# Attention and a two-layer feed-forward on one core: heads of a pair split to float16 together, and a fourth batch moved from float32 to float16 products

## The chip, the cores and the metric

The kernel runs on one core of a Trainium2 chip. A core has a matrix engine (TensorE, PE in the profile, with its weight loads as PEld), a vector engine (VectorE, DVE), a scalar engine (ScalarE, ACT), a general engine (GpSimd, POOL) and SyncE (SP), which here issues every DMA. On-chip memory is SBUF with 128 rows (partitions); TensorE writes its sums to PSUM. The metric is the device time of one execution in microseconds. The kernel before takes 1048.26 us, the median of three runs (1047.59 to 1049.46).

## The reference

Attention over 8 batches, 8 heads, 576 positions and 64 dimensions, with a decay that grows with the positive part of `s`; its result, laid out as 4608 tokens of 512 values, goes through two matrix products with an ELU between them.

```python
scores = scale * np.matmul(q, k.transpose(0, 1, 3, 2))          # scale = 1/8
causal = np.triu(np.ones((S, S), dtype=bool), k=1)
cum = np.cumsum(np.maximum(s, 0.0), axis=-1)
bias = -(cum[:, :, :, None] - cum[:, :, None, :])
scores = np.where(causal, -1000000000.0, scores + np.minimum(bias, 0.0))
scores = scores - np.max(scores, axis=-1, keepdims=True)
attn = np.exp(scores)
attn = attn / (np.sum(attn, axis=-1, keepdims=True) + 1e-09)
x = np.matmul(attn, v)           # then transposed to [4608, 512]
h = x @ w_in                                                     # [512, 2048]
g = np.where(h > 0.0, h, np.exp(np.minimum(h, 0.0)) - 1.0)
out = g @ w_out                                                  # [2048, 512]
```

## The kernel before, in words

**Order of work.** The program records every operation with a priority, the engines that could do it (with a cost in ns for each), what it reads and what it writes. `Plan.issue` then lists the operations greedily: what can start earliest by its own costs goes first, ties go to the priority. So the order on each engine is fixed when the program is built, and each engine waits for semaphores in that order. While TensorE would have nothing to do in the first 60 us of its planned time, the list puts fillers in: transposes into an unused PSUM tile (L1501, `scratch`).

**Two ways through the attention.** Two heads make a pair, so each batch has four pairs. The 576 queries are a first block of 64 and four of 128. `pieces` (L1512) sets the order: the first 320 queries (the first block and blocks 0 and 1) of batches 0 to 3, then batches 4 to 7 whole, then blocks 2 and 3 of batches 0 to 3.

- *The float32 way* (`Low`: `prepare_low` L743, `scoring_low` L770, `weighing_low` L809) serves the first 320 queries of batches 0 to 3, 16 pairs. It loads q, k and v of a pair, multiplies q and k in float32 (L1050), turns the weights of the softmax with TensorE transposes (L818, L834), copies them out of PSUM (L423, L424) and multiplies them with v in float32 (L820, L849).
- *The float16 way* (`Unit`: `prepare` L927, `scoring` L1126, `weighing` L1163) serves the rest. A value is split into a float16 high part and a float16 remainder. A pair is three units here: the first 64 queries of both heads together, then head 0, then head 1. Each unit loads its k and q twice over on 128 rows (tiles `stk`, `stq`), splits them (L408 to L410 for the high part, `remainder` L1008 for the rest), has one DMA to put a copy of q's high part in the tile `q2` (L997) and one to put three rows for the decay under k's remainder (`k2`). The scales come from `group_values` (L867): it loads all of a batch's q and k once more in four pieces of 128x1152 (`sx`, L883 to L889), takes the peaks of them and of the values, and `scales_of` (L620) makes scales of them: DVE maxima, a product with the identity (`flat`, L640), a DVE maximum over it (L632), a product with ones (`every`, L643), and a copy (L645). The scores are two float16 products (`kh` with `qs`, `k2` with `q2`); the weights are turned by DMA transposes (L389, tile `T`) and multiplied with v (`av`, L1212).

In both ways DVE and ACT share the softmax (L1053, L1058), and the result goes by DMA to `x_dram`.

**The feed-forward.** The 4608 tokens go through it in 18 chunks of 256 (`moe_chunk`). A chunk loads its x from `x_dram` (`xc`) and splits it into `xh` (ACT, POOL or DVE, L408 to L410) and `xl` (L1357). Chunk 0 uses float32 products (L1377, L1431); the others take three float16 products in the place of one float32 product: L1381 for the first layer (`h`), 24 matmuls for two of the 16 column blocks, and L1438 for the second (`o`), 12 for two. Chunk 1 holds the end of batch 0's first 320 queries and part of batch 1's, chunk 4 ends those of batch 3, chunk 5 starts with batch 4, and chunks 7, 9 and 11 are the first to need batches 5, 6 and 7.

**Weights.** `load_unit` (L658) brings a 128x512 block as raw words and decodes it with ACT and DVE (L675 to L684), with a peak for each. `weight_scales` (L648) makes one scale for each of the two matrices; its spans in `peaks` are those of the first matrix, those of the second and, as the third, the values' peaks of all 16 float32 pairs (`A_LOW`, `N_CUT * NP + 1`), which the first chunks' x is scaled by. Only then can `split_unit` (L693) make the float16 parts `wp` of the weights, and only with those can chunk 1 start.

**Memory.** The float32 weights' places are used again: the values `va` of the float16 batches stand in the last part of the first group, then in `w_all[0]` and `w_all[1]` by turns; the tiles `T` have `w_all[2]` and `w_all[3]`.

The constants: `P` = 128, `HB` = 64, `CUT` = 2, `NP` = 4 pairs, `N_CUT` = 4, `TMAX` = 256.

## Time and profile before

| | before |
|---|---|
| median of three runs | 1048.26 us |
| profiled execution, its own time | 1049.36 us |
| its span in the trace | 1047.6 us |
| mean granted TensorE clock | 0.996 |
| TensorE busy | 1014.1 us, 97% |
| VectorE busy | 854.6 us, 82% |
| ScalarE busy | 696.6 us, 66% |
| GpSimd busy | 309.2 us, 30% |
| moved by DMA | 169.26 MB |

The profile comes from one execution. A row of the timeline has the start in us, the duration in us, the engine, the line of the program, the operation, the tiles (output, arrow, inputs), the shapes, and in square brackets the engine's idle time before it with the instruction that ended it. Matmul ends are modelled, so a row's duration can reach a little into the next row. A float32 product has two records and a transpose one.

### The profile page before, as it was taken

The numbers are of one execution on the slowest core, as the hardware profiler recorded it, in microseconds if no ns is written. First come the engines' busy times: TensorE is split into PE (matmuls) and PEld (weight loads), VectorE is DVE, ScalarE is ACT, GpSimd is POOL, SyncE is SP. The second block draws the span as 40 slices with busy tenths as digits, with TensorE's granted clock in tenths as the row PEclk, the third lists the DMA queues.
The fourth block names the chain that finished last, engine by engine and source line by source line (L and its number), as shares of the span: only waits on it lengthen the run. The fifth ranks groups of instructions, "written<-read, shape, count | busy, mean of one in ns | idle before, by whom it ended". The sixth has DMA issues, their size and how long they took to land.

```text
span 1047.6 us, 22165 instructions
## 1 busy us (share of the span) xinstructions
PE 1014.1 (97%) x7354; PEld 696.8 (67%) x7354; DVE 854.6 (82%) x2222; ACT 696.6 (66%) x1568; POOL 309.2 (30%) x545
## 2 busy tenths in 40 slices
PE   8879998999999999999999999999999999999998
PEld 7656764666666666666666766666666676767665
DVE  7898656988888988989998999889888888876232
ACT  4788677766776765667777766676666666765343
POOL 6343114123353332335354434123421122210000
PEclk9999999999999999999999999999999999999999
DMA  8999856458889886688758866876785856664000
GB/s 250 251 263 277 250 150 180 129 127 180 188 205 189 171 205 135 147 142 209 158 141 168 215 150 145 175 180 161 156 180 140 154 140 137 145 121 102 6 21 21
DMA packets 289843, 169.26 MB, mean 162 GB/s; under 512 B 205856, under 2 KB 263424, under 8 KB 289728
## 3 DMA queue, kind: packets, MB, share of 16 engines
q1 hardware_dynamic: 289728, 167.84, 68.6%
q8 instruction: 58, 0.95, 0.4%
q14 instruction: 57, 0.47, 0.2%
HBM read 98.99 MB, written 19.24 MB: 113 GB/s over the span
## 4 chain that ended last, share of the span: by engine, by line
PE 50%; DVE 3%; DMA 2%; issue 1%; SPq 1%; POOL 0%; ACT 0%; DVEq 0%; POOLq 0%
PE o L1438 21%; PE h L1381 20%; PE sc L1050 4%; PE av L1212 4%; DVE p L1111 1%; DMA stk<-in_kT_dram 0%; DMA T<-p 0%; DVE h L1413 0%; DVE p L1053 0%; DMA stq_None<-in_qT_dram 0%; SPq L389 0%; DMA stq<-in_qT_dram 0%; DMA q<-qs 0%; DVE qs L1008 0%; DMA xc<-x_dram 0%
## 5 line engine op out<-in xcount | busy, mean ns | idle before, releaser
L1381 PE MATMUL h<-xh,wp 128*128 128x256 f16 x2176 | 397.6, 274 | 6.0 <-DVE wp L699 3.4
L1438 PE MATMUL o<-wp,gg 128*128 128x512 f16 x1632 | 393.8, 379 | 0.0
L1381 PEld LDWEIGHTS <-wp 128*128 128x128 f16 x3264 | 318.7, 98 | 74.5 <-DVE wp L699 5.3
L1381 PE MATMUL h<-xl,wp 128*128 128x256 f16 x1088 | 297.7, 274 | 0.9 <-DVE xl L1357 0.9
L1438 PEld LDWEIGHTS <-gg 128*128 128x128 f16 x1632 | 158.3, 98 | 143.4
L1058 ACT ACTIVATE p<-p,mn 128x192 f32<-128x192 f32 (+1 forms) x224 | 139.7, 624 | 43.7 <-DVE mn L1053 40.8
L1111 DVE SCALAR_TENSOR_TENSOR p<-p,sm,p 128x512 f16<-128x512 f32 (+3 forms) x233 | 149.0, 666 | 5.5 <-ACT p L1107 4.2
L1393 ACT ACTIVATE g<-h,cs 128x512 f32<-128x512 f32 x136 | 93.1, 684 | 90.5 <-PE h L1381 89.8
L1413 DVE SCALAR_TENSOR_TENSOR h<-g,cs,h 128x512 f32<-128x512 f32 x136 | 102.0, 750 | 52.7 <-ACT g L1400 51.4
L1417 ACT ACTIVATE gg<-h 128x512 f16<-128x512 f32 x133 | 78.8, 592 | 60.9 <-DVE h L1413 57.8
L1053 DVE CUSTOM_DVE_ANT_0 p<-sc,maskw 128x192 f32<-128x192 f32 (+1 forms) x224 | 106.0, 484 | 15.4 <-PE sc L1050 10.2
L1420 DVE SCALAR_TENSOR_TENSOR gg<-h,gg 128x512 f16<-128x512 f32 x136 | 93.2, 685 | 18.2 <-ACT gg L1417 17.2
L1103 POOL TENSOR_SCALAR p<-p,sm 128x64 f16<-128x64 f32 (+3 forms) x80 | 52.3, 659 | 144.5 <-DVE sm L1064 68.5
L1107 ACT ACTIVATE p<-p,sm 128x512 f16<-128x512 f32 (+3 forms) x128 | 72.4, 588 | 18.0 <-issue 6.9
L1050 PE MATMUL sc<-kh,qs 128*128 128x192 f16 (+2 forms) x256 | 75.8, 300 | 1.3 <-DVE mn L1053 0.7
L1050 PE MATMUL sc<-k,q 128*128 128x192 f16 (+2 forms) x256 | 75.5, 299 | 0.8 <-DMA q<-qs 0.7
L1212 PEld LDWEIGHTS <-v 128*64 128x64 f16 x896 | 45.4, 110 | 20.2 <-issue 9.8
L1212 PE MATMUL av<-T,v 128*64 128x256 f16 (+5 forms) x896 | 58.6, 280 | 0.2 <-DMA T<-p 0.2
L408 POOL TENSOR_SCALAR v<-va,scales 128x320 f16<-128x320 f32 x37 | 22.4, 611 | 109.4 <-PE av L1212 91.3
L408 POOL TENSOR_SCALAR qs<-stq,scales 128x256 f16<-128x256 f32 (+1 forms) x36 | 25.2, 701 | 91.3 <-PE sc L1050 80.9
L1008 DVE SCALAR_TENSOR_TENSOR k<-stk,scales,kh 64x576 f16<-64x576 f32 x61 | 49.9, 819 | 0.5
L1400 ACT ACTIVATE g<-g 128x512 f32<-128x512 f32 x77 | 48.4, 628 | 2.0
(189 smaller groups left out, 1441.8 us busy)
## 6 DMA issues: line engine op xcount, KB each, us to landing
stk<-in_kT_dram SPq DMA_DIRECT2D x64, 288.0 KB
va<-in_vb_dram SPq DMA_DIRECT2D x32, 320.0 KB
sx<-in_qT_dram SPq DMA_DIRECT2D x32, 288.0 KB
sx<-in_kT_dram SPq DMA_DIRECT2D x32, 288.0 KB
raws<-in_w_in_dram SPq DMA_DIRECT2D x16, 512.0 KB
raws<-in_w_out_dram SPq DMA_DIRECT2D x16, 512.0 KB
out_dram<-ost SPq DMA_DIRECT2D x32, 256.0 KB
stq<-in_qT_dram SPq DMA_DIRECT2D x32, 256.0 KB
```

What stands on the lines that cost most here:

```text
L1050: pe_.matmul(view(sc.v[:, :cw]), l, r, start=n == 0, stop=n == len(pairs) - 1)
L1053: op(prio, [("DVE", 84 + dve_p(cw), lambda i=i, sc=sc: dve.tensor_tensor_reduce(pt.v[:, i * cw : (i + 1) * cw], sc.v[:, :cw], mv(i * cw, c ...
L1058: op(prio, [("ACT", 480 + w / 1.2, lambda: act.activation(pt.v[:, :w], pt.v[:, :w], AF.Exp, bias=mn.v[:, n - 1 : n], scale=-1.0, accum_out ...
L1107: ("ACT", 295 + n / 1.2, lambda part=part: act.activation(part(t16, 0), own(part), AF.Copy, scale=sm.v[:, r])),
L1111: ("DVE-SB", dve_2(n), lambda part=part: dve.scalar_tensor_tensor(part(t16, 1), own(part), sm.v[:, r], part(t16, 0), ALU.mult, ALU.subtract)),
L1212: pe_.matmul(av.v[w.h * HB : (w.h + 1) * HB, dst], w.values.v[:, w.h, kb, v], part(w, kb, m), start=kb == 0 and m == 0 and v == 0, stop=kb ...
L1381: pe_.matmul(columns(k), weight_part(f, 0, part)[1]()[:, c * P : (c + 1) * P], xx.v[:, c], start=(c == 0 and m == 0), stop=(c == NCB - 1 a ...
L1393: op(side, [("ACT", act_c(W) + (0 if native else 90), lambda: act.activation(g.v, hp.v, AF.Exp, scale=1.0 if native else by(3)))], [hp] + ...
L1413: op(side, [("DVE", dve_p(W), lambda: dve.scalar_tensor_tensor(hp.v, g.v, by(2 if sign[0] else 1), hp.v, ALU.mult, ALU.max))], [g, cs], [hp])
L1417: ("ACT", act_c(W), lambda: act.activation(gg.v[:, 0], hp.v, AF.Copy, scale=2.0**-DOWN)),
L1420: op(side, [("DVE", dve_p(W), lambda: dve.scalar_tensor_tensor(gg.v[:, 1], hp.v, 2.0**-DOWN, gg.v[:, 0], ALU.mult, ALU.subtract))], [hp, ( ...
L1438: pe_.matmul(acc[i].v, gg.v[:, g, at], weight_part(f, 1, part)[1](), start=(f == 0 and m == 0), stop=(f == NF - 1 and m == 2),)
```

## The change

1. **`N_LOW = 3`.** Only batches 0, 1 and 2 go the float32 way for their first 320 queries. Batch 3's go the float16 way, as a group of their own, with two query blocks in place of four.
2. **Scales.** Each batch of the float32 way gets a scale for its values by a `scales_of` of its own, and `weight_scales` no longer has the third span. A float16 group needs only its values' scale: the second loads of q and k (`sx`) and their peaks are gone.
3. **Heads of a pair split together.** `prepare_pair` loads a pair's k and q once, head 0 on rows 0 to 63 and head 1 on rows 64 to 127, takes a peak for each row (`pk`), makes a power of two for each row of q and its inverse for k, and splits all with one operation for each part of k and of q. `spread` then puts the parts with twelve DMAs from SBUF to SBUF, and the decay rows with a thirteenth, into a tile `set` with the four operands of the two score products for both heads. There are two such sets in turns; the second has the place of `w_all[1]`, so `va` has `w_all[0]` alone after the first group. `scoring` waits for all parts of the set.

The core of the diff:

```diff
-N_CUT, CUT = 4, 2
+N_CUT, CUT, N_LOW = 4, 2, 3
...
-    groups = [(b, False) for b in range(N_CUT, B)] + [(b, True) for b in range(N_CUT)]
+    groups = [(b, False) for b in range(N_LOW, B)] + [(b, True) for b in range(N_CUT)]
...
-        scales_of(-600, [(A_IN, NF + 1), (A_OUT, NF + 1), (A_LOW, N_CUT * NP + 1)], 0)
+        scales_of(-600, [(A_IN, NF + 1), (A_OUT, NF + 1)], 0)
...
+        if j == NP - 1:
+            scales_of(-600, [(A_LOW + b * (NP + 1), NP + 1)], C_LOW + b)
...
-        home = w_parts[NG - 1] if at == 0 else w_all[(at - 1) % 2]
+        home = w_parts[NG - 1] if at == 0 else w_all[0]
...
-        for kind in range(2):
-            for c in range(2):
-                sx = plan.buf(sb, [P, 2 * S], F32, f"sx_{at}_{kind}_{c}", tag="sx")
...
-                peak(prio, 2 * S, lambda sx=sx: sx.v, [], first + NP + 1 + 3 * kind + c,
-                     aside=lambda sx=sx: sx.v, also=[sx])
-        scales_of(prio, [(first, NP + 1), (first + NP + 1, 3), (first + NP + 4, 3)], col)
+        scales_of(prio, [(first, NP + 1)], col)
...
+    def prepare_pair(u, o):
...
+        peak(prio, w, lambda: sq.v[:, :w], [sq], 0, aside=lambda: unread(w), dst=pk)
+        peak(prio, n, lambda: sk.v[:, :n], [sk], 1, aside=lambda: unread(n), dst=pk)
...
+        op(prio, [("DVE-SB", 350.0, powers)], [(pk, 0), (pk, 1)], [(pk, 2)])
...
+        split(1, n, kp, sk)
+        split(0, w, qp, sq)
...
+        spread(kp, 0, n, top, K1, "kh")
+        spread(kp, 0, n, low, K1, "kh2")
+        spread(qp, 0, w, top, Q1, "qh")
+        spread(qp, 0, w, top, Q2, "qh2")
...
+        spread(kp, 1, n, top, K2, "kl")
+        spread(qp, 1, w, low, Q1, "ql")
...
-        used = [u.kh, u.k2, (u.qs, 0), (u.qs, 1), u.q2]
+        o = u.set
+        used = [(o, part) for part in (
+            "aux", "weights", *((part, h) for part in ("kh", "kh2", "qh", "qh2", "kl", "ql") for h in (0, 1)))]
```

The list that results has on TensorE 134 fillers where there were 181, and on SP 1193 DMAs where there were 909, 208 of them transposes where there were 192.

**TensorE where chunk 1 starts.** The names: `avl_b_j`, `sc_b_j` and `trl_b_j` belong to pair j of batch b in the float32 way, `every_0` is the product that spreads the weights' scales, `h_0_*` and `o_0_*` are chunk 0, `h_1_0` is chunk 1. Before:

```order
L640 MATMUL flat_0_2034<-ident_66,tops_1_145 128x128
L849 MATMUL avl_3_2_1994<-tl_3_2_1988,vs_0_103 64x192 x2
L834 MATMUL trl_3_2_2_2043<-ident_66,p1_84 128x128
L834 MATMUL trl_3_2_2_2043<-ident_66,pl4_3_2_1832 128x128
L1431 MATMUL o_0_1_1385<-wa_3_1514,gg_0_7_1928 128x512
L643 MATMUL every_0_2048<-own_0_2038,all_ones_148 128x3
L849 MATMUL avl_3_2_1994<-tl_3_2_1988,vs_0_103 64x64 x2
L1050 MATMUL sc_3_3_4_0_2055<-kl_3_3_1717,ql_3_3_1836 128x320
L1381 LDWEIGHTS wp_0_2057
L1381 MATMUL h_1_0_2108<-xh_2081,wp_0_2057 128x256
```

In the changed kernel the same product stands in the middle of chunk 0's first layer, behind the third batch's last scores:

```order
L1040 MATMUL sc_2_3_4_0_1557<-kl_2_3_1094,ql_2_3_1310 128x320
L847 MATMUL avl_2_2_1486<-tl_2_2_1481,vs_0_103 64x64 x2
L1379 MATMUL h_0_5_1569<-x0_0_0_464,wa_2_1090 128x256 x2
L1379 MATMUL h_0_5_1569<-x0_0_1_709,wa_2_1090 128x256
L636 MATMUL flat_0_1585<-ident_66,tops_1_145 128x128
L1379 MATMUL h_0_5_1569<-x0_0_1_709,wa_2_1090 128x256
L1379 MATMUL h_0_5_1569<-x0_0_0_464,wa_2_1090 128x256 x2
L639 MATMUL every_0_1605<-own_0_1592,all_ones_151 128x2
L1379 MATMUL h_0_5_1569<-x0_0_1_709,wa_2_1090 128x256
```

The weights' scales moved ahead of the end of chunk 0, and nothing of a fourth float32 batch stands between them and chunk 1; chunk 1's first rows come 42 rows further on, between the second-layer products of chunk 0:

```order
L1379 MATMUL h_0_7_1772<-x0_0_0_464,wa_3_1351 128x256 x2
L1379 MATMUL h_0_7_1772<-x0_0_1_709,wa_3_1351 128x256 x2
L1433 MATMUL o_0_0_1092<-wa_3_1351,gg_0_6_1754 128x512 x2
L1433 MATMUL o_0_1_1205<-wa_3_1351,gg_0_6_1754 128x512 x2
L1383 LDWEIGHTS wp_0_1620
L1383 MATMUL h_1_0_1818<-xh_1797,wp_0_1620 128x256
```

**TensorE where chunk 5 starts.** `av_4_3` is the last pair of batch 4, `sc_5_*` are scores of batch 5, `h_5_0` is the first product of chunk 5. Before, chunk 5 follows right on chunk 4's second layer:

```order
L1438 LDWEIGHTS gg_4_6_4795
L1438 MATMUL o_4_1_4323<-wp_3_2219,gg_4_6_4795 128x512
L1381 LDWEIGHTS wp_0_2057
L1381 MATMUL h_5_0_4847<-xh_2081,wp_0_2057 128x256
L1381 LDWEIGHTS wp_0_2057
L1381 MATMUL h_5_0_4847<-xl_2094,wp_0_2057 128x256
```

In the changed kernel the part of `h_5_0` that needs batch 4's last two pairs stands a few rows behind the last product of that batch:

```order
L1209 MATMUL av_4_3_1_0_4815<-T_4_3_1_0_4723,v_4_3_0_0_3101 64x64
L1040 LDWEIGHTS set_0_194
L1040 MATMUL sc_5_0_1_0_1_0_4855<-set_0_194 128x320
L1040 LDWEIGHTS set_0_194
L1040 MATMUL sc_5_0_1_0_1_0_4855<-set_0_194 128x320
L1168 MATMUL av_5_0_None_0_4867<-pc_5_0_None_0_4773,vs_5_0_None_0_4553 128x128 x2
```

The rest of that stretch is scores of batch 5 alone, up to the product of chunk 5:

```order
L1040 MATMUL sc_5_1_0_0_0_0_4913<-set_1_1832 128x192
L1040 LDWEIGHTS set_1_1832
L1040 MATMUL sc_5_1_0_0_0_0_4913<-set_1_1832 128x192
L1175 MATMUL tr_5_1_None_0_4959<-ident_66,psh_5_1_None_0_4917 128x128
L1383 LDWEIGHTS wp_0_1620
L1383 MATMUL h_5_0_4714<-xh_1797,wp_0_1620 128x256
```

Between the last `av_4_3` and this row now stand 27 rows of TensorE, where 320 stood before; the part of `h_5_0` that needs only the first two pairs stands ahead of both.

**SP where batch 4 is prepared.** Before, one pair's float16 operands take few DMAs, among them the loads of `sx` for the next batch:

```order
L384 DMA q2s_191<-qs_4_1_None_0_2869 64x128
L389 DMA_TRANSPOSE T_4_0_0_0_2855<-p16_4_0_0_0_3_2843 128x9x128
L384 DMA stk_4_1_0_0_2932<-in_kT_dram 128x576
L384 DMA k2_0_291<-aux_dram_455 3x576
L384 DMA stq_4_1_0_0_2941<-in_qT_dram 128x4x128
L384 DMA stk_4_1_1_0_2948<-in_kT_dram 128x576
L384 DMA sx_5_0_1_2953<-in_qT_dram 64x1152
L384 DMA k2_1_327<-aux_dram_455 3x576
L384 DMA sx_5_0_1_2953<-in_qT_dram 64x1152
```

In the changed kernel the parts of the set stand between the outputs of chunk 2 and the x of chunk 4:

```order
L384 DMA set_1_1832<-kp_4_1_None_0_3214 64x576 x4
L384 DMA set_1_1832<-qp_4_1_None_0_3230 64x576 x4
L384 DMA set_1_1832<-kp_4_1_None_0_3214 64x576
L384 DMA out_0_dram<-ost_2_0_3269 128x512
L384 DMA set_1_1832<-kp_4_1_None_0_3214 64x576
L384 DMA xc_4_0_3293<-x_dram_374 128x256 x2
L384 DMA out_0_dram<-ost_2_1_3287 128x512
L384 DMA set_1_1832<-qp_4_1_None_0_3230 64x576 x2
```

Twelve DMAs of the pair's parts now stand in the queue where its three copies of q stood (`q2s` and the two `q2`), and none loads `sx`.

More of the change, by code (lines that the diff above doesn't have):

```diff
@@ L524, in rows @@
                 )
[L526 to L532 removed]
+        op(60, [("Pool-M", 5200.0, rows)], [], [(o, "weights")])
+        op(60, [("Pool-M", 800.0, lambda: pool.memset(o.v[HB:, K2], 0.0))], [], [(o, "aux")])
     def mask_tiles():
@@ L902, in group_values @@
-        op(prio, [("DVE-SB", 450.0, others)], [(scales, col)], [(scales, col + 3)])
+            load(prio + j, lambda j=j: va.v[:, j, :whole], lambda j=j: vb[u.b, j, :, 1 : 1 + whole], [],
+                 [(va, (j, "whole"))], P * whole * D * 4)
+            for rows in HALF[: nv - whole]:
+                load(prio + j, lambda j=j, rows=rows: va.v[rows, j, whole:], lambda j=j: vb[u.b, j, :HB, 1 + whole : 1 + nv],
+                     [], [(va, (j, rows.start))], HB * 2 * D * 4)
+            peak(prio, nv * D, lambda j=j: va.v[:, j], values_of(va, j), first + j, mybir.AxisListType.XY,
+                 aside=lambda: unread(nv * D).rearrange("p (n d) -> p n d", d=D))
@@ L909, in pair_values @@
+        parts = plan.buf(sb, [P, 2, u.last + 2, 2, D], F16, f"v_{u.tag}", tag="v", bufs=N_V)
         by = lambda: scales.v[:, col : col + 1]
@@ L1010, in remainder @@
                 ("Pool", pool_1(size) + pool_2(size), in_place),
-            ], [given, *reads], writes)
-        remainder(w, lambda: u.qs.v[low, :w], lambda: sq.v[low, :w], lambda: u.qs.v[low, :w], 0, low,
-                  [(u.qs, 0)], [sq, (u.qs, 1)])
-        remainder(n, lambda: k_own(u.k2, top), lambda: k_view(st.v[top, :n]), lambda: k_own(u.kh, top), 1, top,
-                  [u.kh], [st, (u.k2, "kl")])
-        if h is not None:
-            return
+            ], [(pk, 2), (t, 0)], [src, (t, 1)])
@@ new lines, in prepare_pair, with spread, dst @@
+        split(1, n, kp, sk)
+        split(0, w, qp, sq)
+        u.w, first = w, (S - w, S)
+        def spread(src, part, size, rows, m, label):
+            for h, own in enumerate(HALF):
+                def dst(h=h):
+                    if m in (K1, K2):
+                        return o.v[rows, m, h, :size]
+                    return o.v[rows, m].rearrange("p h t -> p (h t)")[:, first[h] : first[h] + size]
+                load(prio, dst, lambda own=own: src.v[own, part, :size], [(src, part)], [(o, (label, h))], HB * size * 2)
@@ new lines, in prepare @@
+    def prepare(u):
+        if u.h == 1 or (u.h == 0 and not u.blocks[0]):
+            return
+        turn = pairs_seen[0] % 2
+        pairs_seen[0] += 1
+        if len(pair_sets) == turn:
+            pair_sets.append(plan.buf(sb, [P, 4, 2, S], F16, "set_1", tag=w_all[1].key[1]))
+        if pairs_seen[0] <= 2:
+            weigh(pair_sets[turn])
+        u.set = pair_sets[turn]
+        prepare_pair(u, u.set)
+        if u.h is not None:
+            return
+        b, j, prio = u.b, u.j, u.prio
+        u.vs = plan.buf(sb, [P, 1, 2, D], F32R, f"vs_{u.tag}", tag="vs0")
+        v_src = lambda: vb[b, j, :, 0:1]
@@ L1266, in attention @@
                     pair = pair_values(u, *values)
-                u.values, u.back = pair, values[1] + 3
+                u.values, u.back = pair, values[1] + 1
                 if u.h == 0:
@@ L1271, in attention @@
             prepared(u)
+            if type(u) is Unit and not hasattr(u, "set"):
+                u.set, u.w = operands
+            if type(u) is Unit:
+                operands = u.set, u.w
             if was is Low and was is not type(u):
@@ L1313, in chunk_scales @@
         cols = tuple(sorted({
-            4 + N_SCALES * groups.index((b, late)) if (b, late) in groups else 2 for b, late, *_ in rows}))
+            4 + N_SCALES * groups.index((b, late)) if (b, late) in groups else C_LOW + b for b, late, *_ in rows}))
         if cols in by_columns:
```

199 lines of the change are left out of this document (81 added, 118 removed).

## The prediction

> **What bounds the kernel now.** I read the page first, for the shares of the engines.
>
> ```profile
> span 1047.6 us, 22165 instructions
> PE 1014.1 (97%) x7354; PEld 696.8 (67%) x7354; DVE 854.6 (82%) x2222; ACT 696.6 (66%) x1568; POOL 309.2 (30%) x545
> ```
>
> TensorE is busy for 97% of the span, so what counts is its work and its few gaps. The busy time of each engine by stage (columns: stretch, its length, busy us and instructions of PE, PEld, DVE, ACT, POOL, then the granted clock, the DMA share and GB/s) says where the gaps are.
>
> ```profile
> 0.00:50.00 50.00, 43.01 (x313) 35.52 (x314) 42.16 (x114) 31.35 (x93) 26.70 (x72) 1.00 0.89 243
> 50.00:100.00 50.00, 40.49 (x237) 29.52 (x236) 45.92 (x152) 43.11 (x134) 22.33 (x48) 1.00 1.01 281
> 100.00:150.00 50.00, 50.00 (x252) 34.48 (x251) 31.66 (x86) 35.33 (x97) 6.36 (x19) 1.00 0.73 199
> 150.00:200.00 50.00, 41.86 (x238) 26.18 (x237) 38.50 (x98) 35.59 (x79) 16.53 (x24) 0.93 0.58 159
> 200.00:350.00 150.00, 148.53 (x1079) 99.88 (x1077) 129.00 (x343) 105.64 (x229) 47.13 (x77) 1.00 0.80 178
> 350.00:950.00 600.00, 596.69 (x4590) 408.65 (x4589) 533.29 (x1376) 405.92 (x876) 190.13 (x305) 1.00 0.72 158
> 950.00:1047.00 97.00, 93.50 (x657) 62.61 (x655) 34.05 (x59) 39.70 (x66) 0.00 (x0) 0.99 0.13 37
> ```
>
> There are three regimes. To 100 us the DMA engines are full (0.89, 1.01) and TensorE idles for 16.5 us, with fillers on top. From 150 to 200 it idles for 8.1 us and loses 7% of the clock. From 200 on it is busy for over 99%; what goes there is worth its TensorE time, as long as VectorE (533.29 of 600) and the queues keep ahead.
>
> The hole at 177 us is read from VectorE's timeline, then TensorE's (start, duration, operation, in brackets the idle time before it and what ended it).
>
> ```profile
> 138.50 0.70 DVE L684 SCALAR_TENSOR_TENSOR wa<-raws 128x512 uint32<-128x512 uint32 x1 [0.15 <-ACT raws L675]
> ...
> 168.87 0.62 DVE L606 TENSOR_REDUCE peaks<-vs 128x1 f32<-128x448 f32 x1
> ...
> 173.84 0.16 DVE L645 COPY scales<-every 128x3 f32<-128x3 f32 x1 [0.89 <-PE every L643]
> ```
>
> ```profile
> 177.15 0.27 PE L1381 MATMUL h<-xh,wp 128*128 128x256 f16 x1 [2.35 <-ACT xh L409]
> 178.35 0.27 PE L1381 MATMUL h<-xl,wp 128*128 128x256 f16 x1 [0.93 <-DVE xl L1357]
> 180.55 0.61 PE L1381 MATMUL h<-xh,wp 128*128 128x256 f16 x2 [1.93 <-DVE wp L699]
> 181.16 0.63 PE L1381 MATMUL h<-xh,wp 128*128 128x256 f16 x2
> ...
> 186.34 0.38 PE L1381 MATMUL h<-xh,wp 128*128 128x256 f16 x2
> 190.08 0.39 PE L1381 MATMUL h<-xh,wp 128*128 128x256 f16 x2 [1.46 <-DVE wp L699]
> ```
>
> The last weight is decoded at 138.50, but the weights' scale is copied only at 173.84: its third span waits for the values' peak of the last float32 pair (168.87). Then x, its remainder and the weights' parts are made while TensorE waits 2.35 + 0.93 + 1.93 + 1.46 = 6.7 us, and its clock is halved for a while (0.63 for rows that take 0.38 later): 7% of 50 us is 3.5 us.
>
> **A. TensorE's work for batch 3's first 320 queries.** Rows of a float32 pair, the records of its transposes and products in the first 200 us, the reductions for scales, and the float16 products:
>
> ```profile
> 92.83 1.14 PE L1050 MATMUL sc<-kl,ql 128*128 128x128 f32 x6
> 93.81 0.38 PE L834 MATMUL trl<-ident,p 128*128 128x128 f32 x2
> 94.47 1.24 PE L1050 MATMUL sc<-kl,ql 128*128 128x320 f32 x4
> 95.55 0.27 PE L818 MATMUL trl<-ident,pl 128*128 128x128 f32 x1
> ```
>
> ```profile
> 0.00:200.00 200.00, 21.96 (x210) 14.25 (x210) 6.40 (x24) 5.36 (x21) 0.98 0.80 221
> ```
>
> ```profile
> L640 PE MATMUL flat<-ident,tops 128*128 128x128 f32 x18 | 3.6, 280 | 0.0
> L643 PE MATMUL every<-own,all_ones 128*128 128x3 f32 x18 | 2.9, 232 | 0.6 <-DVE own L636 0.4
> ```
>
> ```profile
> 9.32 6.71 PE L1501 MATMUL scratch<-ident 128*128 128x128 f32 x60
> ```
>
> ```profile
> 513.22 2.62 PE h L1381 x24
> ...
> 590.05 2.59 PE o L1438 x12
> ```
>
> A float32 pair: the scores from start to start are 0.98 and 1.08, less the little that the first waits, 2.0 us; 11 transposes at a filler's 6.71/60 = 0.112 are 1.2; the products with v are 21.96/16 = 1.37 at most (that row is for the tile `avl`; modelled ends overlap), 1.2. Together 4.4, four pairs 17.5. In float16 a column costs 2.62/24/256 = 0.427 ns: two heads by 192 + 320 keys by two products are 2048 columns, 0.87; the first block of 64 queries, which keeps one transpose and float32 products, some 0.5; the products with v some 1,500 columns, 0.65. Together 2.05, four pairs 8.2. There are four reductions for scales more (13, were 9) at (3.6 + 2.9)/9 = 0.72 with overlapping ends, half of that net, 1.4. A = -17.5 + 8.2 + 1.4 = **-7.9**. Ends: the busy time of these groups would make a float32 pair 5 us, -10; with half of it given back in the first 100 us, where TensorE isn't the bound, -4.
>
> **B. The start.** DMA up to 129.5 us (packets and bytes; loads of `sx` in it):
>
> ```profile
> DMA packets 20616, 33.37 MB, mean 258 GB/s; under 512 B 2397, under 2 KB 15873, under 8 KB 20602
> sx<-in_qT_dram SPq DMA_DIRECT2D x12, 288.0 KB
> sx<-in_kT_dram SPq DMA_DIRECT2D x8, 288.0 KB
> ```
>
> Of the 33.37 MB, 20 loads of `sx` (5.8 MB, 22 us at 258 GB/s) go. They are read ahead for later batches, so the transfers that TensorE waits for gain only what stood behind them. The 47 fillers that are no longer listed stood for 5.3 us, but a place without a filler can be a wait. I take **-3** (ends 0 and -8). GpSimd's ones for the old tiles become 5.2 us pieces for the sets by the list's own costs; behind them stand GpSimd's clears of the first pairs' tiles, and should they stand in front it would cost a wait of that size (+5); I take nothing.
>
> **C. The start of chunk 1.** The scale now needs the weights alone, so its reduction can come right behind the decoding and the weights' parts are made while chunk 0 still runs. The 6.7 us of waits and 3.5 us of lost clock go, but for one step of x in front: **-9** (ends -4 and -10). What is late next is x for chunks 3 and 4, now from the float16 way with its longer chain; between batch 3's last product and the rest of chunk 3's first stand some 12 us of TensorE work in the new order, the length of the chain below. I count nothing there.
>
> **D. A new wait at chunk 5.** In the order the rest of its first product stands 27 rows behind batch 4's last product, with 3,328 columns of float16 scores in between, 1.4 us, and a float32 product and a transpose, some 0.5: 1.9 us. What must happen meanwhile is seen where chunk 7 follows batch 5:
>
> ```profile
> 473.89 0.69 ACT L1224 ACTIVATE x_None<-av,scales 128x512 f32<-128x512 f32 x1 [0.48 <-PE av L1212]
> 474.60 0.33 SPq L384 DMA_DIRECT2D x_dram<-x_None  x1
> 479.64 0.53 SPq L384 DMA_DIRECT2D xc<-x_dram  x1
> 483.42 0.72 ACT L409 ACTIVATE xh<-xc,cs 128x512 f16<-128x512 f32 x1 [0.77 <-PE h L1381]
> 485.62 0.74 DVE L1357 SCALAR_TENSOR_TENSOR xl<-xc,cs,xh 128x512 f16<-128x512 f32 x1
> 486.47 0.27 PE L1381 MATMUL h<-xh,wp 128*128 128x256 f16 x1
> ```
>
> From the copy of the output to the product: 486.47 - 473.89 = 12.6 us. Less 1.9 that is **+11**. Queued behind the waiting product on TensorE are all of chunk 5 and the later scores of batch 5. Ends: 0, if batch 4's attention runs ahead of TensorE's work, since then no row waits; and +24, see the second rival.
>
> The clock: the stretch from 50 to 100 us idles for 9.5 us at a clock of 1.00, that from 150 to 200 for 8.1 us at 0.93, so a wait may cost clock or not; I leave it out of D, and the loss of the second row, 3.5 us, stands in the upper end. The Trainium skill ("TensorE: Matmul & The Clock Gate", Part 1: The HAM clock gate) says that the clock halves after an idle window of some 3.4 us and comes back after as long a busy one. The row with 0.93 agrees and the row with 1.00, whose idle time is in pieces, neither agrees nor disagrees. An estimate by that page adds 1.7 us to D, and the time would be 1041.1.
>
> **The sum.** -7.9 - 3 - 9 + 11 = -8.9: a span of 1038.7. The profiled execution took 1049.36 for its span of 1047.6, 1.8 more; the median of the runs, 1048.26, lies 0.7 above the span. 1038.7 + 0.7 = **1039.4**.
>
> Copies, splits and peaks on VectorE, ScalarE and GpSimd: a pair's 12 splits become 4, over twice the rows, and two peaks and four tiny operations come; of GpSimd's 309 us and ScalarE's 697 us some go. None bounds the span as long as TensorE is busy.
>
> **The rivals.**
>
> *1. Chunk 5 does not wait.* The start is gained and attention keeps ahead, since VectorE has 64 us without work per 600 in the steady stretch. Without D: 1047.6 - 7.9 - 3 - 9 = 1027.7, with 0.7 1028.4. Against it: the order's own costs put batch 4's last product right in front. Chance 0.18.
>
> *2. Slower: the queue starves TensorE at each batch.* A float16 pair's SP work becomes 8 transposes and some 26 other DMAs, by these rows (issue time least, median, most in ns):
>
> ```profile
> L389 SPq DMA_TRANSPOSE T<-p x192: 1197/1260/3217, 241.1 to 959.7; - x192
> L384 SPq DMA_DIRECT2D q<-qs x64: 467/476/1351, 191.0 to 937.4; - x64
> ```
>
> 8 x 1.26 + 26 x 0.476 = 22.5 us, and 4 more for the chunks' traffic. TensorE has for a batch 2.25 chunks (8 x 2.62 + 8 x 2.59 = 41.7 each, 94) and some 15 of attention (for each pair 2 x 2 x 1,536 columns of scores, 2.6 us, and 1.2 for the rest), 109 us, 27 a pair. SP is in order, and a set's parts wait for the scores of the pair two before it. From a pair period over 27 us on, each batch ends late: with 29 us, 8 us a batch for batches 5, 6 and 7, whose slack (13 to 16 us of TensorE work by the order) is then gone, and at chunk 5 the whole of the 24: 1039.4 - 11 + 24 + some 11 = 1063. For it: 22.5 + 4 is close to 27. Against: transposes already stand in the same queue with 909 DMAs, and TensorE is busy for 99.4% there. Chance 0.18.
>
> *3. No change.* The TensorE work that goes comes back as waits for attention, which VectorE paces: its work ahead of chunk 5 is hardly less (batch 3's softmax is the same, peaks for each pair come). What C saves is then waited for at chunk 5 and so is A: 1045 to 1050. Chance 0.14, of which 0.03 lie below 1046.2.
>
> *4. The scale does not move.* If chunk 1 starts as late as before, for its x or the weights' parts, there is no D either: 1047.6 - 7.9 + 0.7 = 1040.4. It is held in the forecast's range.
>
> **How the numbers follow.** The forecast holds 0.50, with its own range 1032 to 1045 (D from 4 to 16, clock loss included). About 0.2% (2.1 us) is what a measurement of this kernel can tell from no change. Faster: 0.50 + 0.18 + 0.03 = 0.71; same 0.11; slower 0.18. The range goes from 1024, below the first rival with B at its end, to 1056, which holds the smaller cases of the second rival and leaves out some 0.17 in all.
>
> **What would show it.** Right: the copy of the weights' scale at 125 to 140 us; chunk 1's first product near 150 without waits for `wp`; one wait of about 10 us ahead of chunk 5's first product, ended by `xh` or `xl`, near 360 to 380 us; the stretch after it over 99% busy. A is wrong if TensorE's busy time falls by less than 5 us; C if `every` for the weights still ends the wait; D if no wait over 4 us stands at chunk 5. Waits for parts of the set (scores waiting for DMA) over 10 us in sum, or waits at chunks 7, 9 and 11, would be the second rival, and the forecast would be wrong.

## The result and the profile after

The changed kernel takes 1145.67 us (median of four runs, 1142.85 to 1150.40) where the kernel before takes 1048.86 (1047.59 to 1049.95 in the same comparison). The ratio is 1.0928, with a 95% interval from 1.0888 to 1.0968. The forecast was 1039.4 with a range up to 1056, so it was wrong in sign and far outside its range.

The page of the changed kernel, in the same two lines as that of before:

```profile
span 1141.0 us, 22403 instructions
PE 1035.0 (91%) x7299; PEld 695.8 (61%) x7299; DVE 842.7 (74%) x2361; ACT 676.5 (59%) x1579; POOL 262.0 (23%) x442
```

No engine of the page became fuller in its share: TensorE fell from 97% to 91%, VectorE from 82% to 74%. The span grew by 93.4 us. TensorE's idle time grew from 1047.6 - 1014.1 = 33.5 us to 1141.0 - 1035.0 = 106.0, that is by 72.5, and its busy time by 20.9: its mean granted clock fell from 0.996 to 0.976, and 2% of 1035 us is 21. So the loss is waiting, and clock that is lost beside it. Where it lies is seen in the busy time by stage (stretch, length, then PE, PEld, DVE, ACT, POOL, clock, DMA share, GB/s):

```profile
100.00:150.00 50.00, 48.21 (x219) 29.95 (x218) 44.48 (x127) 37.29 (x91) 13.80 (x23) 1.00 0.38 116
150.00:200.00 50.00, 45.83 (x329) 30.73 (x327) 41.58 (x113) 24.46 (x58) 19.33 (x24) 1.00 0.32 74
200.00:350.00 150.00, 131.86 (x932) 87.45 (x933) 104.14 (x308) 80.48 (x192) 35.81 (x58) 0.97 0.53 126
350.00:950.00 600.00, 540.23 (x3954) 360.75 (x3953) 465.79 (x1306) 364.08 (x829) 137.72 (x209) 0.97 0.68 150
```

Chunk 1 starts at 148.48 instead of 177.15, so the feed-forward is ahead at first. From 350 to 950, where TensorE was busy for 596.69 of 600 us, it is now busy for 540.23, and every other engine is less busy too, the DMA engines among them (0.72 before, 0.68 now). What TensorE waits for, in sum (us, times, longest); the first line is the largest wait of the kernel before, the others are of the changed kernel:

```profile
PE sc L1050 <- DVE mn L1053: 7.5, 10, 2.3
PE sc L1040 <- DVE mn L1043: 26.8, 27, 3.5
PE av L1209 <- DMA T<-p: 26.1, 13, 4.9
PE tr_None L1175 <- POOL psh_None L1061: 8.6, 3, 4.0
```

These are all stages of the attention: scores, turned weights, the turn of the first block. No wait is longer than 4.9 us; they are spread over all steps of a pair. The resource with no time left is one that the page's busy shares leave out, SyncE's queue. Here is all that SyncE issues in the changed kernel from one late pair's output (`x_dram<-x`) to the next (start, time of the issue, DMAs in it):

```profile
808.95 0.53 SPq L384 DMA_DIRECT2D x_dram<-x  x1
809.58 1.76 SPq L384 DMA_DIRECT2D set<-kp  x3
811.43 1.34 SPq L389 DMA_TRANSPOSE T<-p  x1
812.82 0.59 SPq L384 DMA_DIRECT2D set<-kp  x1
813.46 2.51 SPq L384 DMA_DIRECT2D set<-qp  x4
816.02 0.46 SPq L384 DMA_DIRECT2D set<-aux_dram  x1
816.53 1.10 SPq L384 DMA_DIRECT2D set<-kp  x2
817.67 1.24 SPq L384 DMA_DIRECT2D set<-qp  x2
818.95 1.35 SPq L384 DMA_DIRECT2D stq<-in_qT_dram  x2
820.34 1.24 SPq L384 DMA_DIRECT2D stk<-in_kT_dram  x2
821.68 2.66 SPq L389 DMA_TRANSPOSE T<-p  x2
824.60 0.41 SPq L384 DMA_DIRECT2D out_dram<-ost  x1
825.06 0.92 SPq L384 DMA_DIRECT2D xc<-x_dram  x2
826.08 1.17 SPq L384 DMA_DIRECT2D out_dram<-ost  x2
827.35 1.35 SPq L384 DMA_DIRECT2D stq<-in_qT_dram  x2
828.79 1.82 SPq L384 DMA_DIRECT2D stk<-in_kT_dram  x2
830.67 1.05 SPq L384 DMA_DIRECT2D xc<-x_dram  x2
831.82 1.41 SPq L389 DMA_TRANSPOSE T<-p  x1
833.65 0.33 SPq L384 DMA_DIRECT2D x_dram<-x  x1
```

The 18 rows ahead of the last sum to 22.9 us of the 24.7 us between the outputs: the queue is never idle for long, and most rows begin about a tenth of a microsecond behind the end of the one above. (Loads of k and q for two pairs stand in it, so it is more than one pair's share.) A stretch of the kernel before from one such output to the next:

```profile
790.66 0.52 SPq L384 DMA_DIRECT2D x_dram<-x  x1
791.72 1.28 SPq L389 DMA_TRANSPOSE T<-p  x1
793.09 0.40 SPq L384 DMA_DIRECT2D k<-aux_dram  x1
793.59 0.47 SPq L384 DMA_DIRECT2D q<-qs  x1
794.16 0.53 SPq L384 DMA_DIRECT2D stq<-in_qT_dram  x1
794.75 0.45 SPq L384 DMA_DIRECT2D stk<-in_kT_dram  x1
797.10 2.77 SPq L389 DMA_TRANSPOSE T<-p  x2
803.40 0.26 SPq L384 DMA_DIRECT2D k<-aux_dram  x1
803.85 0.47 SPq L384 DMA_DIRECT2D q<-qs  x1
804.57 0.40 SPq L384 DMA_DIRECT2D stq<-in_qT_dram  x1
805.41 0.33 SPq L384 DMA_DIRECT2D stk<-in_kT_dram  x1
806.38 0.33 SPq L384 DMA_DIRECT2D x_dram<-x  x1
```

There the issues take 7.9 us of 15.7. Both are single stretches, this one a calm one. Over 350 to 950 us, all rows of SyncE summed, the changed kernel has 702 DMAs with 515.7 us of issues (86% of the 600) and 45.7 us in gaps under 0.2 us between them, which leaves 38.6 us; the kernel before has 558 DMAs with 397.1 us (66%) and 37.8 us of such gaps, which leaves 165. The rows by tile give the prices (least, median, most in ns):

```profile
L384 SPq DMA_DIRECT2D set<-kp x96: 461/587/1493, 694.5 to 1024.5; - x96
L384 SPq DMA_DIRECT2D set<-qp x96: 467/595/1177, 697.5 to 1025.8; - x96
```

A DMA that fills a set takes 0.59 us to issue, where the prediction had taken 0.476 from the copy of q.

### The profile page after: what moved, and what is told of

It reads as the page before. It is cut to its first block, busy times and chain, and to the rows that moved or that the text cites. A ratio compares the mean times of both kernels' runs of the same rounds, so it can differ in the third digit from the quotient of the medians.

```text
span 1141.0 us, 22403 instructions
## 1 busy us (share of the span) xinstructions
PE 1035.0 (91%) x7299; PEld 695.8 (61%) x7299; DVE 842.7 (74%) x2361; ACT 676.5 (59%) x1579; POOL 262.0 (23%) x442
## 4 chain that ended last, share of the span: by engine, by line
PE 35%; DVE 10%; DMA 8%; SPq 6%; issue 4%; ACT 3%; POOL 0%; DVEq 0%; ACTq 0%; POOLq 0%
PE h L1383 15%; PE o L1440 13%; SPq L384 5%; PE sc L1040 3%; PE av L1209 3%; DMA T<-p 2%; DMA stq<-in_qT_dram 2%; DMA x_dram<-x_None 2%; DVE p L1043 2%; DVE p L1101 2%; SPq L389 1%; DVE h L1415 1%; ACT g L1395 1%; DMA va<-in_vb_dram 1%; DMA stq_None<-in_qT_dram 1%
## 5 line engine op out<-in xcount | busy, mean ns | idle before, releaser
L1383 PE MATMUL h<-xh,wp 128*128 128x256 f16 x2176 | 408.3, 276 | 2.5 <-DVE gg L1422 1.7
L1101 DVE SCALAR_TENSOR_TENSOR p<-p,sm,p 128x512 f16<-128x512 f32 (+3 forms) x268 | 159.1, 618 | 28.7 <-ACT p L1097 24.1
L1048 ACT ACTIVATE p<-p,mn 128x192 f32<-128x192 f32 (+1 forms) x232 | 143.6, 619 | 39.3 <-DVE mn L1043 37.8
L1093 POOL TENSOR_SCALAR p<-p,sm 128x512 f16<-128x512 f32 (+3 forms) x96 | 63.9, 670 | 335.5 <-DMA T<-p 113.2
L1040 PE MATMUL sc<-set 128*128 128x288 f16 (+3 forms) x544 | 114.2, 303 | 28.2 <-DVE mn L1043 26.1
L1097 ACT ACTIVATE p<-p,sm 128x512 f16<-128x512 f32 (+3 forms) x148 | 82.8, 574 | 53.3 <-DMA T<-p 32.7
L1040 PEld LDWEIGHTS <-set 128*128 128x128 f16 x584 | 55.3, 99 | 77.6 <-issue 40.6
L1209 PE MATMUL av<-T,v 128*64 128x256 f16 (+5 forms) x960 | 69.8, 288 | 28.0 <-DMA T<-p 26.1
L408 POOL TENSOR_SCALAR v<-va,scales 128x320 f16<-128x320 f32 (+1 forms) x42 | 23.6, 565 | 92.0 <-PE av L1209 89.3
L1048 ACT ACTIVATION_READ_ACCUMULATOR p<-p,mn 128x1 f32 x232 | 43.7, 188 | 0.0
L1406 DVE TENSOR_SCALAR g<-g 128x512 f32<-128x512 f32 x64 | 28.1, 439 | 19.2 <-ACT g L1395 18.9
```

Source lines behind the costliest of these rows:

```text
L1040: pe_.matmul(view(sc.v[:, :cw]), l, r, start=n == 0, stop=n == len(pairs) - 1)
L1048: op(prio, [("ACT", 480 + w / 1.2, lambda: act.activation(pt.v[:, :w], pt.v[:, :w], AF.Exp, bias=mn.v[:, n - 1 : n], scale=-1.0, accum_out ...
L1097: ("ACT", 295 + n / 1.2, lambda part=part: act.activation(part(t16, 0), own(part), AF.Copy, scale=sm.v[:, r])),
L1101: ("DVE-SB", dve_2(n), lambda part=part: dve.scalar_tensor_tensor(part(t16, 1), own(part), sm.v[:, r], part(t16, 0), ALU.mult, ALU.subtract)),
L1209: pe_.matmul(av.v[w.h * HB : (w.h + 1) * HB, dst], w.values.v[:, w.h, kb, v], part(w, kb, m), start=kb == 0 and m == 0 and v == 0, stop=kb ...
L1383: pe_.matmul(columns(k), weight_part(f, 0, part)[1]()[:, c * P : (c + 1) * P], xx.v[:, c], start=(c == 0 and m == 0), stop=(c == NCB - 1 a ...
```

## The experiments

Four theories stood against each other. **S**: the time that SyncE needs to issue, on one queue in order, paces the attention. **L**: the latency of one pair through the two sets and the split tiles paces it. **F**: the fourth batch's move is what costs. **O**: the order is at fault, since the list prices an issue at 430 ns. The kernel before took 1048.7 to 1049.4 us (medians) beside these runs.

### The fourth batch stays in float32

```diff
-N_CUT, CUT, N_LOW = 4, 2, 3
+N_CUT, CUT, N_LOW = 4, 2, 4
```

> One part undone: N_LOW = 4, so the fourth batch's first 320 queries stay in float32, and the heads are still split together. Theory S (the issuing engine SyncE paces the attention: about 43 of every 50 us are issue time, at 0.59 us for a DMA of the set and 0.62 for a load of q): four short pairs with some 17 us of issue each go and four float32 pairs with some 3 us come, so 30 to 58 us of the 97 lost come back, 1088 to 1116 us. Rival F (the fourth batch's move is what costs, the heads' split is harmless): 1040 to 1055. Rival L (the latency from a load through the two sets to the scores paces each pair): four pairs of some 20 us less, 1075 to 1125, so this run does not tell S from L, only both from F.

Measured: 1151.32 us, ratio 1.0975 (1.0952 to 1.0997). F falls: without the move the kernel is 5.6 us slower than with it. The intervals of the two ratios overlap, so the 5.6 us are not clear of noise; the heads' split together carries the whole loss. The gain of 30 to 58 us that S had expected did not come in the time of the kernel. The traces show it in the attention: the last pair's output is issued at 1013.61 us, where the changed kernel has it at 1065.51, 52 us later. But chunk 1 begins only at 187.96 (148.48 in the changed kernel), so the feed-forward starts 39.5 us later, and 138 us of this run's span lie behind the last pair's output, where the changed kernel has 75. From 350 to 950 us the queue is as full as in the changed kernel, 85% in issues.

### The scales alone

```diff
-        scales_of(-600, [(A_IN, NF + 1), (A_OUT, NF + 1), (A_LOW, N_CUT * NP + 1)], 0)
+        scales_of(-600, [(A_IN, NF + 1), (A_OUT, NF + 1)], 0)
...
+        if j == NP - 1:
+            scales_of(-600, [(A_LOW + b * (NP + 1), NP + 1)], C_LOW + b)
```

This is made to the kernel before, with four such batches.

> The kernel before with one edit alone: a scale for the values of each of the first four batches, and the weights' scale without the third span. Term C of the prediction: chunk 1 starts some 10 us earlier and its waits and its halved clock go: 1037 to 1044 us. Rival: chunk 1 starts earlier, but attention of batch 4 is then late for chunk 5 and takes it back: 1046 to 1050.

Measured: 1050.47 us, ratio 1.0020 (1.0010 to 1.0029): no gain, and slightly slower. The mechanism is there, since the weights' scale comes 30 us earlier and chunk 1 starts at 169.15 instead of 177.15:

```profile
143.77 0.15 DVE L647 COPY scales<-every 128x2 f32<-128x2 f32 x1
```

The gain isn't. In the busy time by stage of this run:

```profile
50.00:100.00 50.00, 38.58 (x224) 29.51 (x222) 44.76 (x151) 40.90 (x125) 18.80 (x44) 0.93 1.00 276
...
150.00:200.00 50.00, 47.74 (x284) 31.24 (x284) 44.29 (x124) 38.78 (x94) 6.83 (x18) 1.00 0.52 145
200.00:350.00 150.00, 146.15 (x1076) 98.59 (x1073) 122.89 (x332) 104.46 (x227) 55.73 (x96) 1.00 0.79 181
```

From 150 to 200 the idle time falls from 8.1 to 2.3 us and the clock is whole; but from 50 to 100 1.9 us more are idle and the clock is 0.93 there instead, and from 200 to 350 the idle time grows from 1.5 to 3.9 us. The hole moved, but not to where the rival had it, at chunk 5: from 350 on this run idles no more than the kernel before (2.6 us of 600 against 3.3).

### The set's DMAs merged

```diff
-        spread(kp, 0, n, top, K1, "kh")
         spread(kp, 0, n, low, K1, "kh2")
-        spread(qp, 0, w, top, Q1, "qh")
-        spread(qp, 0, w, top, Q2, "qh2")
-        spread(kp, 1, n, top, K2, "kl")
+        spread(qp, 0, w, top, Q1, "qh")
+        spread(kp, 0, n, top, K1, "kl", [(kp, 0), (kp, 1)])
```

In it `qh` now fills Q1 and Q2 with one DMA a head, and `kl` brings both parts of k to K1 and K2 with one.

> The changed kernel with the same bytes to the same places in 8 DMAs a pair where it has 12 (k's high and low part for the upper rows in one, q's high part to both of its places in one), 144 issues fewer in all. Theory S: 144 times 0.6 to 0.67 us = 86 to 96 us less issue time, less what a DMA of twice the size takes longer to issue: 1050 to 1105 us. Theory L (latency through the two sets): same bytes, same waits, same sets: 1138 to 1150.

Measured: 1085.52 us, ratio 1.0344 (1.0324 to 1.0364). 60 us come back for 144 issues, 0.42 us each, with the same bytes in the same places. That speaks for S and against L. The price of an issue hardly goes with the size: in that run's late pairs a merged DMA of k takes 605 ns (median), the single one beside it 541.

### Idle DMAs in the changed kernel, and in the kernel before

```diff
+        for m in range(4):
+            load(prio, lambda m=m: idle.v[:HB, m], lambda m=m: kp.v[:HB, 0, m * HB : (m + 1) * HB],
+                 [(kp, 0)], [(idle, m)], HB * HB * 2)
```

> The changed kernel with four more DMAs a pair, 144 in all, of 64 rows by 128 bytes into a tile that nobody reads. Theory S: each costs its issue, 0.35 to 0.67 us, so 50 to 96 us more: 1195 to 1240 us. Theory L: 1.2 MB more and no wait on them: 1143 to 1155.

Measured: 1192.03 us, ratio 1.1366 (1.1346 to 1.1386). The added DMAs cost 46.4 us, 0.32 each, though nothing waits for their data and they are small. L falls again; S had expected 50 or more, so a part of their issue time still found room. In the kernel before:

> The kernel before with the same kind of idle DMAs, four for each of the 32 pairs of heads that go the float16 way with separate heads, 128 in all. In the changed kernel 144 of them cost 46 us, 0.32 each. Theory S: the queue of the kernel before has time to spare (32 to 35 us of issue in 50), so most of the 41 us is hidden: 1048 to 1064 us. Rival (a DMA more costs its price in any kernel, by the transfers or the completions): 1085 to 1095.

Measured: 1073.57 us, ratio 1.0234 (1.0200 to 1.0269): 24 us, 0.19 each, between the two expectations. The queue of the kernel before isn't free either: its issues take 66% of the time from 350 to 950. A likely reason for the cost at that load, not shown by a run, is that the queue is in order, so an issue more delays what stands behind it whenever that is due.

### The set's DMAs from ScalarE

```diff
-                load(prio, dst, lambda own=own: src.v[own, part, :size], [(src, part)], [(o, (label, h))], HB * size * 2)
+                op(prio, [("ACT", 100.0, lambda dst=dst, own=own: nc.scalar.dma_start(dst(), src.v[own, part, :size]), LAG, HB * size * 2)],
+                   [(src, part)], [(o, (label, h))])
```

> The changed kernel with the twelve DMAs of each set issued by ScalarE in place of SyncE; same bytes, same sets, same waits. Theory S: 432 times 0.65 us leave SyncE's queue, which then has about 35 us of issue in 50 as before: 1030 to 1085 us, the upper end if ScalarE, busy for 59%, has to spend 0.6 us for each. Theory L (latency through the two sets): 1138 to 1150.

Measured: 1220.50 us, ratio 1.1635 (1.1589 to 1.1681), 75 us slower still. S, as it stood, missed this. (This version also has the list count 100 ns for such an issue, so its order was made with far too low a price.) ScalarE's timeline of that run shows why the queue wasn't relieved but moved:

```profile
510.68 0.60 ACT L1420 ACTIVATE gg<-h 128x512 f16<-128x512 f32 x1 [1.13 <-DVE h L1416]
510.74 4.03 ACTq L977 DMA_DIRECT2D set<-qp_None  x4
514.81 0.69 ACT L1396 ACTIVATE g<-h,cs 128x512 f32<-128x512 f32 x1 [3.54 <-issue]
```

Four issues take 4.03 us, and the next operation of the feed-forward stands behind them in ScalarE's queue. TensorE then waits for ScalarE's results (in that run):

```profile
PE o L1441 <- ACT gg L1420: 34.8, 14, 7.9
```

In the changed kernel that wait was 1.5 us. The wait of scores for VectorE's `mn` is longer still in this run, 44.3 us where it was 26.8. The Trainium skill ("DMA: Bandwidth & Descriptors", Rules for kernel authors) says of spreading DMAs over issuing engines that it does not help the bandwidth and only saves sequencer issue time. No run here measured the bandwidth part; the issue time is saved on SyncE and paid on ScalarE, whose work is on TensorE's path. Eight merged DMAs from ScalarE:

> The eight merged DMAs a pair, issued by ScalarE. Theory S: SyncE has less to issue than in the kernel before, ScalarE 288 issues: 1025 to 1060 us, and under 1048 if what the prediction counted for TensorE (A and B, 11 us) comes out. Theory L: 1138 to 1150.

Measured: 1165.06 us, ratio 1.1107 (1.1079 to 1.1134): better than twelve from ScalarE by 55, worse than eight from SyncE by 80, and again far above what S had expected.

### The price of an issue in the list

```diff
-SP_COST = 430.0
+SP_COST = 620.0
```

> The changed kernel with the list's price of a DMA issue at 620 ns in place of 430 (the trace has 590 for a set's DMA, 620 to 650 for a load of q). Theory S: another order of the same issues, SyncE is as full: 1125 to 1155 us. Rival O (the order is at fault, since it was made with too low a price): 1060 to 1110.

Measured: 1115.78 us, ratio 1.0639 (1.0610 to 1.0668), 30 us less than the changed kernel and between the two expectations. So O holds for a part: the same DMAs in an order made with a truer price cost less. Together with the merged DMAs:

> The eight merged DMAs a pair (alone: 60 us less than the changed kernel) and the list's price of an issue at 620 ns (alone: 30 less). Theory S with its addition (the queue is full, and a list that thinks an issue cheaper than it is puts too much ahead of what is due): the two add up in part, 1052 to 1072 us. If the price only mattered because the queue was full: 1075 to 1090.

Measured: 1081.58 us, ratio 1.0308 (1.0286 to 1.0329). Only 4 us on top of the merging, so the two don't add up. In the kernel before:

> The kernel before with the list's price of an issue at 620 ns in place of 430. Its own issues take 430 to 500 ns and its queue has time to spare, so by S with its addition: 1045 to 1055 us. Rival (the price is a general lever, the list is better with a higher one whatever the queue holds): 1015 to 1040.

Measured: 1039.55 us, ratio 0.9904 (0.9878 to 0.9931), a gain of 9.3 us. Here the rival was right: the price is a lever in the kernel before as well. With the scales added:

> The kernel before with the price at 620 ns (1039.6 us alone) and the weights' scale without the third span (1050.5 alone, where the earlier start was given back between 200 and 350 us). If it was given back because the attention of batch 4 had no lead, and the price gives it that: 1030 to 1036. If the start never counts: 1037 to 1043.

Measured: 1041.02 us, ratio 0.9918 (0.9899 to 0.9937). The earlier start of chunk 1 gains nothing here either.

### A third tile for the split parts

```diff
-        kp, qp = (plan.buf(sb, [P, 2, S], F16, f"{m}p_{u.tag}", tag="qs", bufs=2) for m in "kq")
+        kp, qp = (plan.buf(sb, [P, 2, S], F16, f"{m}p_{u.tag}", tag="qs", bufs=3) for m in "kq")
```

> The changed kernel with three tiles in turns, where it has two, for the split k and q of a pair (kp, qp), so that the next pair's k can be split before this pair's q has left. Same DMAs. Theory L (a pair's chain waits for the tiles of the pair before): 1090 to 1130 us. Theory S (issue time on the one in-order queue): 1135 to 1152.

Measured: 1157.47 us, ratio 1.1025 (1.0982 to 1.1067). That is above both expectations. The float32 way's q has its tiles from the same place, and this version gives it a third one too; chunk 1 starts at 170.67 in this run, 22 us later than in the changed kernel, while the last pair's output is issued 18 us earlier, at 1047.16. So the run isn't a clean test: more room for the chain gains nothing in the whole, and may be worth some of those 18 us to the attention. A third set was not tried.

### Half of the set by copies, fewer loads, and both

Six of the twelve DMAs of a pair have source and destination on the same rows. They become copies on the engines:

```diff
+                if rows == own:
+                    rounded(prio, size, dst, lambda own=own: src.v[own, part, :size], [(src, part)], [(o, (label, h))])
+                    continue
```

> The changed kernel with six of a pair's twelve DMAs replaced by copies on GpSimd, ScalarE or VectorE: those whose source and destination lie on the same rows (head 0's four to the upper rows, head 1's two to the lower). 216 issues fewer, the price in the list as it was. Theory S: 216 times 0.67 = 145 us of SyncE's time go; at the 0.4 to 0.6 us of time for each 0.67 that the merged DMAs gave: 1055 to 1090 us. Rival E (the work on the other engines around a pair, peaks and splits, is what paces it): more of that work, 1145 or more.

Measured: 1063.54 us, ratio 1.0130 (1.0106 to 1.0153). 82 us for 216 issues, 0.38 each, with the price at 430. Rival E falls: the other engines took the copies with time to spare. Copies also shorten a pair's chain, so this run alone doesn't tell S from L.

Then, on top of the merged DMAs and the price of 620, k and q laid out in memory by pair, so that a load covers both heads:

```diff
-        for m, rows in enumerate(HALF):
-            load(prio, lambda m=m, rows=rows: sk.v[rows, :n], lambda m=m: kT[b, :HB, 2 * j + m, :n], [], [(sk, m)], HB * n * 4)
+        load(prio, lambda: sk.v[:, :n], lambda: kS[b, j, :, :n], [], [sk], P * n * 4)
```

> Merged DMAs, true price, and k and q laid out in memory so that a full pair's k comes in one DMA where it has two and its q in one where it has four (late pairs: one and two). 88 issues fewer than with the merged DMAs and the true price (1081.6 us). Theory S: 88 times 0.7 = 62 us of SyncE's time: 1040 to 1065. If a floor other than the queue stands under it: 1072 to 1085.

Measured: 1040.01 us, ratio 0.9907 (0.9885 to 0.9929). 41.6 us for 88 issues, 0.47 each, and the kernel is faster than the kernel before, but not than the kernel before with the price of 620 (1039.55). With the copies added:

> The two before together: merged, true price, few loads, and the four DMAs of a pair that stay on their rows as copies. SyncE then has fewer issues than in the kernel before. Theory S: the time falls to what TensorE's work and the kernel before's own lead allow, 1015 to 1045 us. If a floor other than the queue stands under it: 1060 or more.

Measured: 1028.74 us, ratio 0.9806 (0.9781 to 0.9832). This version beats both kernels, and by 1% the kernel before with the price of 620. SyncE issues 817 DMAs, fewer than the 909 of the kernel before, though their issues take about as long (406.5 us from 350 to 950, against 397.1); the page of this version, and the busy time by stage, show no floor under the queue at 1060:

```profile
PE 1002.4 (98%) x7315; PEld 690.5 (67%) x7315; DVE 855.7 (83%) x2388; ACT 710.9 (69%) x1634; POOL 334.6 (33%) x579
```

```profile
200.00:350.00 150.00, 150.00 (x1131) 102.38 (x1130) 132.32 (x372) 111.21 (x252) 53.11 (x88) 1.00 0.66 143
350.00:950.00 600.00, 592.80 (x4548) 405.86 (x4547) 524.24 (x1453) 425.38 (x935) 200.91 (x326) 0.99 0.69 147
```

TensorE is busy for 742.80 of 750 us from 200 to 950 (745.22 in the kernel before), and the two largest waits of the changed kernel have shrunk: scores wait 6.3 us in all for `mn`, and the products with the turned weights 0.2. The last 144 issues gave only 11 us, 0.08 each; with TensorE busy for 98% of the span there was little more to gain.

The next table has the share of the 600 us from 350 to 950 that SyncE's issues take in each profiled execution.

| kernel | DMAs that SyncE issues | price in the list | share in issues | us |
|---|---|---|---|---|
| idle DMAs added | 1337 | 430 | 89% | 1192.0 |
| changed | 1193 | 430 | 86% | 1145.7 |
| changed | 1193 | 620 | 87% | 1115.8 |
| merged | 1049 | 430 | 83% | 1085.5 |
| merged | 1049 | 620 | 83% | 1081.6 |
| half by copies | 977 | 430 | 78% | 1063.5 |
| merged, fewer loads | 961 | 620 | 79% | 1040.0 |
| merged, fewer loads, copies | 817 | 620 | 68% | 1028.7 |
| before | 909 | 430 | 66% | 1048.9 |
| before | 909 | 620 | 66% | 1039.6 |

## Why the prediction was wrong

**The step that failed** is the weighing of the second rival, "22.5 + 4 is close to 27", which got a chance of 0.18. The forecast's own sum has no term for SyncE's issues at all; it counts TensorE's time "as long as VectorE (533.29 of 600) and the queues keep ahead". (600 less that 533.29 is 66.7, not the 64 of the first rival; nothing hangs on it.) The second rival named the right mechanism, SyncE's queue, and the wrong size, in three ways.

- *The price and the gap.* It took 0.476 us for each of the new DMAs, from the row of the copy of q. The set's DMAs take 0.587 and 0.595. What differs is the neighbour and not the tile: with idle DMAs in the kernel before, the copy of q still took 475 ns, and the idle DMAs that stand in rows right behind it 594, though they are smaller. Behind each issue there is also a gap of 0.05 to 0.1 us, which was left out. For a full pair the dearer price is offset by fewer DMAs than were counted. From 350 to 650 us, with the loads of ten pairs, SyncE has 84 transposes and 259 other DMAs, 258.7 us of issues: 25.9 a pair, where the prediction has 26.5. With 23.1 us of short gaps it is 28.2, over the 27 that TensorE needs. So the sum was near, and "close to 27" lay on the wrong side of it.
- *The place.* It worked the sum for full pairs only. A late pair (blocks 2 and 3) has half the transposes but the same twelve DMAs for its set, and these are 16 of the 36 pairs. From 694 to 1026 us, where their sets are filled, the issues sum to 281.2 us and the short gaps to 24.7: 19.1 us a pair. In the kernel before the outputs of the late pairs come 17.7 us apart on average (701.93 to 967.11), in the changed kernel 19.6 (771.69 to 1065.51).
- *The consequence.* It priced a late batch as one stall of some 24 us at chunk 5 and a little at three more chunks, 1063 in all. A full queue costs in every pair: 56 us more of idle time from 350 to 950 alone, and clock. The first full pair's output of batch 4 is issued at 306.21 us instead of 265.69, 41 us later, since batch 3 now goes through the queue ahead of it (with batch 3 left in float32 it is issued at 239.01); the last late pair's comes 98 us later.

The other steps:

- **A**, less work on TensorE, 7.9 us: the changed kernel does not show it. Busy time times mean clock is 1014.1 x 0.996 = 1010.0 before and 1035.0 x 0.976 = 1010.2 after. It shows in the last version, at a clock of 0.996: TensorE's busy time falls from 1014.1 to 1002.4. That version has 150 fillers where there were 181, 3.5 us at 0.112 each; the other 8.2 us are near the 7.9.
- **B**, the start, 3 us: the idle time of the first 100 us fell from 16.5 to 8.3 us (42.31 and 49.38 busy, fillers included). That is 8.2 us, more than counted and just past its end of 8.
- **C**, the start of chunk 1, 9 us: the scale was to come at 125 to 140 us and came at 125.82 (its copy on VectorE); chunk 1 was to start near 150 and started at 148.48. The signs were right and the value was wrong: made alone, the same edit gave nothing (1050.47), since the idle time went to other places.
- **D**, a wait ahead of chunk 5: it is there, near 400 us, but not for the cause that was named. TensorE's timeline of the changed kernel at that place:

```profile
389.66 3.97 PE L1209 MATMUL av<-T,v 128*64 128x512 f16 x27 [4.91 <-DMA T<-p]
...
402.58 0.37 PE L1383 MATMUL h<-xh,wp 128*128 128x256 f16 x1 [0.42 <-DVE xh L410]
403.77 0.37 PE L1383 MATMUL h<-xl,wp 128*128 128x256 f16 x1 [0.81 <-DVE xl L1359]
```

The long wait is that of batch 4's own attention for its turned weights; the split of x ends only 0.42 + 0.81 us. The prediction had named waits for parts of the set as the second rival's sign; they sum to under 5 us. The lateness showed at the transposes, which stand in the same queue, and at the scores, which wait for VectorE's `mn`. How that second wait comes from the queue was not followed step by step; what ties it to the issues is that it goes with their number: 45.8 us with the idle DMAs added, 26.8 in the changed kernel, 18.7 with the merged DMAs, 13.0 with half of them as copies, 6.3 in the last version.

- **The clock** was left out of D. The busy time by stage around one wait of the changed kernel (3.49 us, ended at 452.84) shows it: a stretch of three microseconds from ahead of it and one from behind it.

```profile
443.00:446.00 3.00, 3.00 (x29) 2.52 (x27) 2.86 (x7) 1.89 (x5) 2.68 (x4) 1.00 0.58 135
453.00:456.00 3.00, 3.00 (x18) 2.17 (x18) 2.83 (x11) 1.40 (x4) 0.00 (x0) 0.56 0.88 169
```

TensorE is busy throughout both, but at a clock of 0.56 behind the wait, and does 18 matmuls where it did 29. The rule of the Trainium skill ("TensorE: Matmul & The Clock Gate", Part 1: The HAM clock gate), that an idle window of some 3.4 us halves the clock, agrees with this row. Other rows of this case don't fit it: a wait of 2.35 us that ended at 489.62 was followed by a clock of 0.50 from 490 to 493, one of 3.52 us that ended at 720.25 by a clock of 1.00, and in the kernel before the lower clock behind 177.15 followed waits of 2.35 and 0.93 us, so the prediction's row with 0.93 doesn't show the rule either. The length of one wait doesn't decide it here. In the trace of the changed kernel 11 stretches at half clock, 54.6 us together, make up the mean of 0.976; up to its last 2 us the kernel before has one, of 6.8 us.

What stays open: why the price of 620 helps the kernel before, whose own issues mostly take under 500 ns, was not told apart. That the order is better with it was measured; what in the order does it was not. About half of the gain lies from 150 to 200 us, where TensorE is busy for 47.32 us instead of 41.86. Open too is where an issue spends its time: from ScalarE it takes as long as from SyncE, and no run tells whether the issuing engine or what takes the DMA from it sets the 0.59 us.
